# Four buffers for block 0 of the probabilities, and a narrower tile for the last two key blocks of P^T

## The chip, the cores and the metric

The kernel runs on one core of one Trainium2 chip. The metric is the device time of one execution in microseconds (us). The core has a matrix engine (PE, with the loading of its weights as a row of its own, PEld), a vector engine (DVE), a scalar engine (ACT), a general engine (POOL) and a queue that issues DMAs (SP). Each engine works through its own list of instructions in order and waits on semaphores for the others.

## The reference

Block-causal attention over 8 batches x 8 heads, 576 positions, head dimension 64, and then one feed-forward layer over the 4608 tokens whose activation is a rational function.

```python
scores = 1/sqrt(64) * q @ k.T                      # per head, 576 x 576
mask   = (i // 64) >= (j // 64)                    # blocks of 64
attn   = exp(scores - max); attn /= attn.sum + 1e-9
x      = (attn @ v) as 4608 x 512
h = x @ w_in                                       # 512 -> 2048
P = a0 + a1 h + a2 h^2 + a3 h^3
Q = 1 + |b0||h| + |b1| h^2
out = (P / (Q + 1e-6)) @ w_out                     # 2048 -> 512
```

All of it is float32. The kernel keeps that accuracy by splitting each operand into a high and a low part (names ending in h and l, of the type fp32r) and by summing three products of them, so every matrix product appears three times on PE.

## The kernel before

**Attention** goes through 32 visits, one for each pair of heads (8 batches x 4 pairs). A visit has five row blocks t = 0 to 4 with 64, 128, 128, 128, 128 queries that see 64, 192, 320, 448, 576 keys. For each t and each of the two heads, `scores` (L414 to L441) multiplies q by k on PE and takes the row maxima on DVE; where t > 0 a matmul of 64 columns (L436) adds the mask to the last 64 keys. `expo` (L443) takes the exponential on ACT (L449), and when both heads are there POOL scales the rows by 1/sum: keys 0 to 63 of both heads go to a small tile `pk` (L458, "block 0"), the other keys stay in place (L462).

`transp` (L466 to L488) transposes the probabilities on PE in groups of blocks, one PSUM bank a group (L481). From each group ACT copies the high part (L486) and DVE takes the low part (L487) into tiles that live through the whole attention: `pt0` (block 0 of t = 0, 1, 2), `pt1` (blocks 1 to 4 of t = 1, 2) and `pt2` (blocks 0 to 8 of t = 3, 4: nine key blocks by 256 queries, the first 128 of t = 3 and the second 128 of t = 4). The queries of t = 3 see 448 keys, which are blocks 0 to 6; for blocks 7 and 8 their columns are zeroed once at the start (L323) and stay zero.

`pv` (L490) multiplies V by these tiles. Its second group (g = 1) is nine key blocks by three products, 27 matmuls of 256 columns, six of them on blocks 7 and 8 (L500). ACT and DVE split the result (L503, L504), and a DMA writes it to DRAM as x.

**The feed-forward part** is cut in two passes. The first does 10 of the 16 slices of the inner dimension for 18 chunks of 256 tokens, five units a chunk: unit `c_u` is unit u of chunk c. In a unit, `first` makes 24 matmuls (L207), then ACT, POOL (L216, L217) and DVE evaluate P and Q, `recip` and `split` end in gh on ACT (L239) and gl on POOL (L240), and `second` makes 12 matmuls with these as weights (L257). The second pass does the other six slices for chunks of 512 tokens and runs after attention.

**Order.** The program emits attention item by item and feed-forward steps between them by a fixed count. What emits first has priority, but the list that each engine gets is settled by the framework's scheduler, which places an instruction when, on its own timeline, its inputs are there and its tile has a free buffer. `pk` has two buffers (L420): the pk of row block t can be written only after the transposes of the row block two before it have read theirs, and `transp` follows its row block by 9 or 10 items, about a visit.

Of the kernel before, what the change touches and what calls it, by code (L numbers as in the profile page):

```python
# [9 lines left out]
F32 = mybir.dt.float32  # L10
F32R = mybir.dt.float32r
# [50 lines left out]
def attn_ffn_kernel(  # L62
# [11 lines left out]
    nc = tc.nc  # L74
# [32 lines left out]
    b0, b1 = bab[:, 0:1], bab[:, 1:2]  # L107
# [197 lines left out]
    Q0 = [0, 64, 192, 320, 448]  # L305
# [3 lines left out]
    with ExitStack() as actx:  # L309
        ps_a = actx.enter_context(tc.tile_pool(name="ps_a", bufs=5, space=PSUM))  # L310
        att = actx.enter_context(tc.tile_pool(name="att", bufs=2))
        apers = actx.enter_context(tc.tile_pool(name="apers", bufs=1))


        pt0 = [apers.tile([128, 1, 320], F32R, name=f"pt0{x}") for x in "hl"]
        pt1 = [apers.tile([128, 4, 256], F32R, name=f"pt1{x}") for x in "hl"]
        pt2 = [apers.tile([128, 9, 256], F32R, name=f"pt2{x}") for x in "hl"]

        vpad = [apers.tile([128, 128 + 4 * 192], F32R, name=f"vp{x}") for x in "hl"]
        for x in pt1:  # L320
            nc.vector.memset(x[:, 2:4, 0:128].bitcast(F32), 0.0)
        for x in pt2:
            nc.vector.memset(x[:, 7:9, 0:128].bitcast(F32), 0.0)  # L323
        for x in vpad:
            nc.vector.memset(x.bitcast(F32), 0.0)

# [69 lines left out]
        def vblock(x, b):  # L396
            c = 0 if b == 0 else 128 + 192 * ((b - 1) // 2) + 64 * ((b - 1) % 2)
            return x[:, c:c + 128]
# [3 lines left out]
        def bank(p, name):  # L402

            if p < LEND:
                nbank[0] += 1
                pool, tag = ((ps_a, "a"), (ps_o, "o0"), (ps_o, "o1"), (ps_h, "a"))[nbank[0] % 4]
            else:
                pool, tag = ps_a, "a"
            return pool.tile([128, 512], F32, name=name, tag=tag)

        def pieces(t):
            return [(0, NK[t])] if t < 4 else [(0, 288), (288, 288)]

        def scores(p, t, j):  # L414
            s = st_[p]
            nq = NQ[t]
            if j == 0:
                pt = att.tile([128, 2, NK[t]], F32, name=f"p{p}_{t}", tag=f"p{t}", bufs=1)

                pk = att.tile([128, 2, 64], F32, name=f"pk{p}_{t}", tag="pk", bufs=2) if t > 0 else pt  # L420
                nm = att.tile([128, 2, 2], F32, name=f"nm{p}_{t}", tag="nm", bufs=4)
                sm = att.tile([128, 2, 2], F32, name=f"sm{p}_{t}", tag="sm", bufs=4)
                s[t] = (pt, pk, nm, sm)
            pt, pk, nm, sm = s[t]
            kq = s["kq", j]
            qs = slice(Q0[t], Q0[t] + 128)
            banks = []
            for i, (c0, w) in enumerate(pieces(t)):
                ww = max(w, 256)
                ps = ps_a.tile([128, 512], F32, name=f"s{p}_{t}_{j}_{i}", tag="a")  # L430
                last = t > 0 and c0 + w == NK[t]
                nc.tensor.matmul(ps[:, :ww], lhsT=kq[:, 0, qs], rhs=kq[:, 1, c0:c0 + ww], start=True, stop=False)  # L432
                nc.tensor.matmul(ps[:, :ww], lhsT=kq[:, 0, qs], rhs=kq[:, 2, c0:c0 + ww],  # L433
                                 start=False, stop=not last)
                if last:
                    nc.tensor.matmul(ps[:, w - 64:w], lhsT=mrow, rhs=mcol, start=False, stop=True)  # L436
                nc.vector.reduce_max(out=nm[:nq, j, i:i + 1], in_=ps[:nq, :w], axis=AX.X, negate=True)  # L437
                banks.append(ps)
            if t == 4:
                nc.vector.tensor_tensor(out=nm[:, j, 0:1], in0=nm[:, j, 0:1], in1=nm[:, j, 1:2], op=ALU.min)  # L440
            s[t, j] = banks  # L441
# [24 lines left out]
        def transp(p, t):  # L466
            pt, pk, _, _ = st_[p].pop(t)
            nq = NQ[t]
            nb = 1 + 2 * t
            groups = {1: [1], 3: [1, 2], 5: [1, 4], 7: [4, 3], 9: [3, 3, 3]}[nb]  # L470
            blk = 0
            for gi, gn in enumerate(groups):
                ps = bank(p, f"t{p}_{t}_{gi}").rearrange("p (c t) -> p c t", c=4)
                for i in range(gn):
                    x = blk + i
                    if x == 0:
                        src = pk[:nq].rearrange("q j k -> q (j k)")
                    else:
                        key = 64 + 128 * ((x - 1) // 2)
                        src = pt[:nq, (x - 1) % 2, key:key + 128]  # L480
                    nc.tensor.transpose(ps[:, i, :nq], src, ident[:nq, :nq])  # L481
                (hi, lo), b0, c0 = ((pt2, blk, Q0[t] - 320) if t > 2 else (pt0, 0, Q0[t]) if blk == 0 else
                                    (pt1, blk - 1, Q0[t] - 64))
                dh = hi[:, b0:b0 + gn, c0:c0 + nq]
                dl = lo[:, b0:b0 + gn, c0:c0 + nq]
                nc.scalar.copy(out=dh, in_=ps[:, :gn, :nq])  # L486
                nc.vector.tensor_tensor(out=dl, in0=ps[:, :gn, :nq], in1=dh.bitcast(F32), op=ALU.subtract)  # L487
                blk += gn  # L488

        def pv(p, g):  # L490
            b, hp = divmod(visits[p][0], NPAIR)
            vh, vl = vpad
            nb, w = ((5, 320), (9, 256))[g]
            o = ps_a.tile([128, 512], F32, name=f"o{p}_{g}", tag="a")
            for x in range(nb):
                s0 = 64 if (g == 0 and x > 0) else 0
                hi, lo = ((y[:, x] for y in pt2) if g else (y[:, 0] for y in pt0) if x == 0 else
                          (y[:, x - 1] for y in pt1))
                for i, (vv, pp) in enumerate(((vh, lo), (vh, hi), (vl, hi))):
                    nc.tensor.matmul(o[:, s0:w], lhsT=vblock(vv, x), rhs=pp,  # L500
                                     start=(x == 0 and i == 0), stop=(x == nb - 1 and i == 2))
            xs = att.tile([128, 2, 320], F32R, name=f"x{p}_{g}", tag="xs", bufs=1)
            nc.scalar.copy(out=xs[:, 0, :w], in_=o[:, :w])  # L503
            nc.vector.tensor_tensor(out=xs[:, 1, :w], in0=o[:, :w], in1=xs[:, 0, :w].bitcast(F32), op=ALU.subtract)  # L504
            nc.sync.dma_start(out=xscr[b][:, hp, :, g * 320:g * 320 + w], in_=xs[:, :, :w].bitcast(F32))
# [7 lines left out]
        def attn_steps():  # L513
# [8 lines left out]
            for k in range(len(items) + ALAG2 + ALAG3 + 8):  # L522
                for x in [x for x in todo if x[0] == k]:
                    todo.remove(x)
                    x[1](*x[2])
                if k < len(items):
                    p, t, j = items[k]
                    ts = visits[p][1]
                    if (t, j) == (ts[0], 0):
                        if p + 1 < NV:  # L530
                            o0, o1, o2 = OFFS[len(ts)]
                            at(k + o0, load, p + 1)
                            at(k + o1, prep, p + 1, 0)
                            at(k + o2, prep, p + 1, 1)
                    at(k + ALAG2, expo, p, t, j)
                    if j == 1:
                        lag = min(ALAG3, nxt[k] - 1)
                        at(k + lag, transp, p, t)
                        if t in (2, 4):
                            at(k + lag + 1, pv, p, t // 4)  # L540
                            if t == ts[-1] and p + 1 < NV:
                                at(k + lag + 1, vprep, p + 1)
                    scores(p, t, j)
                yield k
# [87 lines left out]
```

## Time and profile before

| | |
|---|---|
| median of 3 runs | 1382.86 us (1381.88 to 1384.80) |
| profiled execution, its own time | 1380.84 us |
| its span in the trace | 1379.1 us |
| instructions in it | 24416 |
| PE, weight load busy | 1278.1, 1149.6 us |
| DVE, ACT, POOL busy | 1027.2, 909.4, 958.2 us |
| granted PE clock, mean | 0.974 |
| DMA | 200.84 MB, mean 146 GB/s |

The profile is of one execution. A row of a group reads: line, engine, operation, output<-input, sizes and count, then busy us and mean ns of one, then idle time of the engine just before these instructions and what ended it. A row of the waits reads: who waited <- for whom, us in total, times, longest. A row of the chain or of the timeline begins with its start and its us. In names, the numbers of buffers are left out.

### The profile page before, as it was taken

What the parts mean: (1) busy time and instruction counts of PE and PEld (TensorE: products, weight loads), DVE (VectorE), ACT (ScalarE), POOL (GpSimd) and SP (SyncE); (2) the same over time, 40 slices, a digit from 0 to 9 for tenths busy, and PEclk for the clock granted to TensorE, in tenths of its full rate; (3) what the DMA queues carried; (4) which work ended last, traced back from release to release, by engine and by line L of the source; (5) the groups of instructions that cost most, each with busy time, mean ns of one, the idle gap of its engine ahead of it and who ended that gap; (6) DMA issues with size and microseconds to landing.
All of it is one profiled execution on the core that took longest, in us unless ns stands there. A gap on an engine that the chain in (4) does not pass through costs nothing.

```text
span 1379.1 us, 24416 instructions
## 1 busy us (share of the span) xinstructions
PE 1278.1 (93%) x8088; PEld 1149.6 (83%) x8088; DVE 1027.2 (74%) x2048; ACT 909.4 (66%) x2250; POOL 958.2 (69%) x1240
## 2 busy tenths in 40 slices
PE   4677899999899979999999999999989999999997
PEld 3667788999888879888998999998979888888885
DVE  5898877787778857887767777776676767676675
ACT  4766767777677756777767777776645655555553
POOL 4889987687678747777767676666556666666654
PEclk9788999999999999999999999999999999999999
DMA  9778556666556655665654555652632233333332
GB/s 216 198 196 238 146 150 166 168 166 181 148 145 150 164 151 132 165 166 153 157 140 123 154 134 122 160 127 65 213 141 77 77 123 123 122 123 123 122 113 86
DMA packets 216925, 200.84 MB, mean 146 GB/s; under 512 B 129504, under 2 KB 184800, under 8 KB 216800
## 3 DMA queue, kind: packets, MB, share of 16 engines
q1 hardware_dynamic: 216736, 199.28, 53.6%
q8 instruction: 65, 1.06, 0.3%
q14 instruction: 60, 0.49, 0.1%
q0 software_dynamic: 64, 0.00, 0.0%
HBM read 98.57 MB, written 44.04 MB: 103 GB/s over the span
## 4 chain that ended last, share of the span: by engine, by line
PE 69%; DVE 9%; POOL 9%; DMA 5%; ACT 3%; issue 3%; SPq 1%; POOLq 0%; DVEq 0%; ACTq 0%
PE h L207 25%; PE o L257 24%; PE o L500 8%; PE t L481 4%; PE s L432 3%; PE s L433 2%; PE tp L366 2%; POOL gl L240 1%; POOL p L462 1%; DMA x<-xscr 1%; POOL u L217 1%; DVE v L231 1%; DVE nm L437 1%; POOL v L216 1%; DMA xscr<-x 1%
## 5 line engine op out<-in xcount | busy, mean ns | idle before, releaser
L207 PE MATMUL h<-x,wih 128*128 128x256 f32 (+1 forms) x1872 | 415.7, 313 | 9.0 <-DMA x<-xscr 7.9
L207 PEld LDWEIGHTS h<-x,wih 128*128 128x128 f32 x1872 | 309.7, 191 | 29.1 <-issue 6.6
L207 PE MATMUL h<-x,wil 128*128 128x256 f32 (+1 forms) x936 | 290.7, 311 | 0.0
L240 POOL TENSOR_TENSOR gl<-s,gh 128x512 fp32r<-128x512 f32 x144 | 188.8, 1313 | 106.4 <-ACT gh L239 103.0
L257 PE MATMUL o<-woh,gl 128*128 128x512 f32 x576 | 232.2, 403 | 12.1 <-POOL gl L240 10.6
L257 PE MATMUL o<-wol,gh 128*128 128x512 f32 x576 | 227.7, 396 | 0.0
L257 PE MATMUL o<-woh,gh 128*128 128x512 f32 x576 | 227.7, 395 | 0.0
L437 DVE TENSOR_REDUCE nm<-s 128x1 f32<-128x288 f32 (+4 forms) x384 | 161.7, 427 | 78.4 <-PE s L436 45.2
L449 ACT ACTIVATE p<-s,nm 128x288 f32<-128x288 f32 (+4 forms) x384 | 184.9, 485 | 48.3 <-DVE nm L437 35.0
L217 POOL TENSOR_TENSOR u<-v,u 128x512 f32<-128x512 f32 x144 | 189.6, 1317 | 9.8
L216 POOL TENSOR_SCALAR v<-u,bab 128x512 f32<-128x512 f32 x144 | 118.9, 826 | 98.1 <-ACT u L214 94.6
L207 PEld LDWEIGHTS h<-x,wil 128*128 128x128 f32 x936 | 178.7, 191 | 8.7
L462 POOL TENSOR_SCALAR p<-p,rc 128x128 f32<-128x128 f32 (+3 forms) x256 | 164.8, 655 | 29.6 <-DVE rc L457 27.7
L218 DVE TENSOR_TENSOR s<-s,h 128x512 f32<-128x512 f32 x144 | 98.5, 684 | 100.1 <-ACT s L215 99.4
L432 PE MATMUL s<-kq 128*128 128x256 f32 (+3 forms) x384 | 137.3, 360 | 24.3 <-DMA kq<-hl 8.9
L224 ACT ACTIVATE v<-u,qcb 128x512 f32<-128x512 f32 x144 | 104.6, 726 | 69.6 <-POOL u L217 68.9
L214 ACT ACTIVATE u<-h 128x512 f32<-128x512 f32 x144 | 85.9, 596 | 94.2 <-PE h L207 90.1
L239 ACT CAST gh<-s 128x512 fp32r<-128x512 f32 x144 | 89.2, 623 | 82.1 <-DVE s L232 81.5
L257 PEld LDWEIGHTS o<-woh,gl 128*128 128x128 f32 x576 | 109.2, 190 | 35.5 <-POOL gl L240 14.3
L257 PEld LDWEIGHTS o<-wol,gh 128*128 128x128 f32 x576 | 109.1, 189 | 22.2
L257 PEld LDWEIGHTS o<-woh,gh 128*128 128x128 f32 x576 | 109.3, 190 | 18.9
L433 PE MATMUL s<-kq 128*128 128x256 f32 (+3 forms) x384 | 120.1, 315 | 0.0
(105 smaller groups left out, 3043.5 us busy)
## 6 DMA issues: line engine op xcount, KB each, us to landing
kq<-hl SPq DMA_DIRECT2D x64, 432.0 KB, 4.3
kq<-hl SPq DMA_DIRECT2D x64, 288.0 KB, 5.3
x<-xscr SPq DMA_DIRECT2D x56, 256.0 KB, 4.2
xscr<-x SPq DMA_DIRECT2D x32, 320.0 KB, 4.7
qr<-in_q_dram SPq DMA_DIRECT2D x64, 144.0 KB, 2.9
kr<-in_k_dram SPq DMA_DIRECT2D x64, 144.0 KB, 3.0
kq<-hl SPq DMA_DIRECT2D x64, 144.0 KB, 4.8
pscr<-os SPq DMA_DIRECT2D x18, 512.0 KB, 2.9
```

The lines of the kernel that those rows point to most:

```text
L207: nc.tensor.matmul(h[:, j, :], lhsT=w[:, dc, fs], rhs=xs[dc][:, hl, :], start=(dc == 0 and i == 0), stop=(dc == 3 and i == 2))
L216: nc.gpsimd.tensor_scalar(out=vt, in0=ut, scalar1=b1, scalar2=b0, op0=ALU.mult, op1=ALU.add)
L217: nc.gpsimd.tensor_tensor(out=ut, in0=vt, in1=ut, op=ALU.mult)
L224: nc.scalar.activation(out=vt, in_=ut, func=AF.Ln, bias=qcb)
L240: nc.gpsimd.tensor_tensor(out=gl.rearrange("p j t -> p (j t)"), in0=st, in1=gh.rearrange("p j t -> p (j t)").bitcast(F32), op=ALU.subtract)
L257: nc.tensor.matmul(self.o[m], lhsT=g[:, j, ms], rhs=w[:, f, :], start=(u == 0 and j == 0 and i == 0), stop=(u == nu - 1 and j == NBU[ph] - ...
L432: nc.tensor.matmul(ps[:, :ww], lhsT=kq[:, 0, qs], rhs=kq[:, 1, c0:c0 + ww], start=True, stop=False)
L433: nc.tensor.matmul(ps[:, :ww], lhsT=kq[:, 0, qs], rhs=kq[:, 2, c0:c0 + ww], start=False, stop=not last)
L437: nc.vector.reduce_max(out=nm[:nq, j, i:i + 1], in_=ps[:nq, :w], axis=AX.X, negate=True)
L449: nc.scalar.activation(out=pt[:nq, j, c0:c0 + w], in_=banks[i][:nq, :w], func=AF.Exp, bias=nm[:nq, j, 0:1], scale=1.0, accum_out=sm[:nq, j ...
L462: nc.gpsimd.tensor_scalar(out=pt[:nq, jj, 64:n], in0=pt[:nq, jj, 64:n], scalar1=rc[:nq, jj:jj + 1], scalar2=1.0, op0=ALU.mult, op1=ALU.mult)
L500: nc.tensor.matmul(o[:, s0:w], lhsT=vblock(vv, x), rhs=pp, start=(x == 0 and i == 0), stop=(x == nb - 1 and i == 2))
```

## The change

`pk` gets four buffers. `pt2` shrinks to the seven blocks that both row blocks use, and blocks 7 and 8 get a tile `pt3` of 128 columns, those of t = 4; the two memsets of zeros go. The transposes of t = 4 are grouped 4, 3, 2 so that the last group is what goes to `pt3`. `pv` takes blocks 7 and 8 from `pt3` with 128 columns that add to the second half of its result. Per partition, `pt2` and `pt3` together hold 2 KB less than `pt2` did, and `pk` 1 KB more.

```diff
-        pt2 = [apers.tile([128, 9, 256], F32R, name=f"pt2{x}") for x in "hl"]
+        pt2 = [apers.tile([128, 7, 256], F32R, name=f"pt2{x}") for x in "hl"]
+        pt3 = [apers.tile([128, 2, 128], F32R, name=f"pt3{x}") for x in "hl"]
...
-        for x in pt2:
-            nc.vector.memset(x[:, 7:9, 0:128].bitcast(F32), 0.0)
...
-                pk = att.tile([128, 2, 64], F32, name=f"pk{p}_{t}", tag="pk", bufs=2) if t > 0 else pt
+                pk = att.tile([128, 2, 64], F32, name=f"pk{p}_{t}", tag="pk", bufs=4) if t > 0 else pt
...
-            groups = {1: [1], 3: [1, 2], 5: [1, 4], 7: [4, 3], 9: [3, 3, 3]}[nb]
+            groups = {1: [1], 3: [1, 2], 5: [1, 4], 7: [4, 3], 9: [4, 3, 2]}[nb]
...
-                (hi, lo), b0, c0 = ((pt2, blk, Q0[t] - 320) if t > 2 else (pt0, 0, Q0[t]) if blk == 0 else
+                (hi, lo), b0, c0 = ((pt3, 0, 0) if blk == 7 else (pt2, blk, Q0[t] - 320) if t > 2 else (pt0, 0, Q0[t]) if blk == 0 else
...
-                s0 = 64 if (g == 0 and x > 0) else 0
-                hi, lo = ((y[:, x] for y in pt2) if g else (y[:, 0] for y in pt0) if x == 0 else
-                          (y[:, x - 1] for y in pt1))
+                pt, b0, s0 = (((pt2, x, 0) if x < 7 else (pt3, x - 7, 128)) if g else
+                              (pt0, 0, 0) if x == 0 else (pt1, x - 1, 64))
+                hi, lo = (y[:, b0] for y in pt)
```

The scheduler also settles a new order on every engine. Three places of it follow; the lines from L500 on are one higher in the changed kernel, and the last number of a name counts tiles.

The first is POOL in the second visit, one piece of the difference: `rc` is 1/sum of a row block (the number behind the name is t), `sm` the sums, `wao`, `wai`, `wil` and `wol` belong to the splitting of the weights, `vpl` is the low part of V.

```order
 L458 TENSOR_TENSOR pk_2_467<-p_2_466,rc_2_535 128x128
 L462 TENSOR_SCALAR p_2_466<-p_2_466,rc_2_535 128x256 x2
+L458 TENSOR_TENSOR pk_3_542<-p_3_541,rc_3_575 128x128
 L462 TENSOR_SCALAR p_3_541<-p_3_541,rc_3_575 128x384 x2
 L145 TENSOR_TENSOR wil_143<-wpi_2_2_1416,wai_2_2_1414 128x2x256
 L394 TENSOR_TENSOR vpl<-vr_204,vph 128x4x64 x2
+L130 TENSOR_SCALAR wao_2_1458<-wao_2_1458 128x512
 L455 TENSOR_TENSOR sm_4_584<-sm_4_584 128x2
-L458 TENSOR_TENSOR pk_3_542<-p_3_541,rc_3_575 128x128
```

The pk of t = 3 now stands right behind the row block before it, ahead of its own p rows; before, it stood behind them and behind rows of the weights and of V.

The second is PE at the last visit's transposes of t = 4 (`t_4_0`, `t_4_1`, `t_4_2` are the three groups, `h_14_1` and `h_15_1` feed-forward units). Before:

```order
L481 MATMUL t_3_1_13441<-ident,p_3_13098 128x128
L481 MATMUL t_4_0_13485<-ident,pk_4_13177 128x128
L481 MATMUL t_4_0_13485<-ident,p_4_13176 128x128 x2
L481 MATMUL t_4_1_13491<-ident,p_4_13176 128x128 x3
L481 MATMUL t_4_2_13497<-ident,p_4_13176 128x128 x3
L207 MATMUL h_15_1_13875<-x_15_0_13751,wih_142 128x256 x2
```

And in the changed kernel:

```order
L481 MATMUL t_3_1_13441<-ident,p_3_13098 128x128 x3
L481 MATMUL t_4_0_13485<-ident,pk_4_13177 128x128
L481 MATMUL t_4_0_13485<-ident,p_4_13176 128x128 x3
L481 MATMUL t_4_1_13492<-ident,p_4_13176 128x128 x3
L207 MATMUL h_14_1_13556<-x_14_1_13345,wih_142 128x256
L207 MATMUL h_14_1_13556<-x_14_1_13345,wil_143 128x256
L481 MATMUL t_4_2_13498<-ident,p_4_13176 128x128 x2
```

The groups hold 4, 3 and 2 blocks instead of 3, 3 and 3, and the feed-forward unit beside them is an earlier one.

The third is PE at the last P·V of all (`o_1`), with the second product of a feed-forward unit ahead of it (`o_14_1` is the sum of chunk 14; the numbers of gl and gh name the unit). Before:

```order
L257 MATMUL o_14_1_13738<-woh_144,gl_14_3_13817 128x512
L257 MATMUL o_14_1_13738<-woh_144,gh_14_3_13816 128x512
L257 MATMUL o_14_1_13738<-wol_145,gh_14_3_13816 128x512
L500 MATMUL o_1_13520<-pt2l,vph 128x256
L500 MATMUL o_1_13520<-pt2h,vph 128x256
L500 MATMUL o_1_13520<-pt2h,vpl 128x256
```

And in the changed kernel, where the six matmuls on blocks 7 and 8 come apart from the other 21:

```order
L257 MATMUL o_14_1_13738<-woh_144,gl_14_0_13608 128x512
L257 MATMUL o_14_1_13738<-woh_144,gh_14_0_13607 128x512
L257 MATMUL o_14_1_13738<-wol_145,gh_14_0_13607 128x512
L501 MATMUL o_1_13520<-pt3l,vph 128x128
L501 MATMUL o_1_13520<-pt3h,vph 128x128
L501 MATMUL o_1_13520<-pt3h,vpl 128x128
```

The last P·V now stands behind unit 14_0, three units earlier than before.

## The prediction

> **What bounds the kernel now.** I read three views in this order: busy time by stage, the chain that ended last, and the waits of the engine that the chain names. First the stages: up to 200 us (attention alone, with the weights being split), 200 to 1000 (attention mixed with the first pass of the feed-forward part), and the rest (feed-forward alone). Columns: stretch and its length, then busy us and instructions of each engine, granted clock, DMA share, GB/s.
>
> ```profile
> core 0: us, PE busy (x) PEld busy (x) DVE busy (x) ACT busy (x) POOL busy (x), PEclk, DMA share, GB/s
> 0.00:200.00 200.00, 145.47 (x905) 131.30 (x906) 162.92 (x373) 133.90 (x385) 163.00 (x218) 0.87 0.76 193
> 200.00:1000.00 800.00, 767.59 (x5489) 712.93 (x5487) 606.64 (x1311) 569.71 (x1534) 570.91 (x827) 1.00 0.59 150
> 1000.00:1379.00 379.00, 365.07 (x1698) 305.39 (x1698) 257.62 (x366) 205.79 (x332) 224.29 (x196) 0.98 0.33 112
> ```
>
> From 200 us on PE is busy 96% of the time at full clock; in the first stage DVE and POOL are busier (163 of 200) than PE (145). So PE work taken away counts after 200 us and hardly before, and of PE's idle time only 800 - 767.6 = 32.4 us is there to be won in the middle stage. The chain says the same:
>
> ```profile
> PE 69%; DVE 9%; POOL 9%; DMA 5%; ACT 3%; issue 3%; SPq 1%; POOLq 0%; DVEq 0%; ACTq 0%
> PE h L207 25%; PE o L257 24%; PE o L500 8%; PE t L481 4%; PE s L432 3%; PE s L433 2%; PE tp L366 2%; POOL gl L240 1%; POOL p L462 1%; DMA x<-xscr 1%; POOL u L217 1%; DVE v L231 1%; DVE nm L437 1%; POOL v L216 1%; DMA xscr<-x 1%
> ```
>
> The P·V matmuls (L500) are 8% of it, so a cheaper L500 shows in the end; POOL is 9%.
>
> **Part 1: six matmuls of each second P·V group stream 128 columns, not 256.** What a 256-column matmul costs is the step from start to start, not its recorded duration (the records overlap). PE's timeline (start, duration):
>
> ```profile
> 806.24 0.19 PE L436 MATMUL s<-mcol,mrow 128*128 128x64 f32 x1
> 806.26 0.36 PE L500 MATMUL o<-pt2l,vph 128*128 128x256 f32 x1
> 806.47 0.28 PE L500 MATMUL o<-pt2h,vph 128*128 128x256 f32 x1
> 806.58 0.29 PE L500 MATMUL o<-pt2h,vpl 128*128 128x256 f32 x1
> ...
> 808.38 0.28 PE L500 MATMUL o<-pt2h,vpl 128*128 128x256 f32 x1
> ```
>
> From 806.47 to 808.38 are 16 steps: 0.12 us each. A 128-column matmul on fp32r data is not in the trace. The nearest row is L436 with 64 columns: from its start to the second L500 is 0.23 us, and one 256-column step of that is 0.12, so 64 columns cost 0.11. A quarter of the columns saves a twelfth of the time: under 256 columns something other than streaming sets the step, in a stream of fp32r matmuls with a new weight each. So 128 columns lie between 0.11 and 0.12, and the gain between 0 and 0.01 us each; I take 0.01, the row it is nearest to in kind. How many count, from the group in the stage 200 to 1000:
>
> ```profile
> L500 PE MATMUL o<-pt2l,vph 128*128 128x256 f32 x234 | 68.1, 291 | 0.3 <-ACT p L449 0.3
> ```
>
> 234 / 9 key blocks = 26 of the 32 visits. 26 x 6 x 0.01 = **1.6 us** less. The six visits before 200 us give nothing, since PE has 54 us to spare there.
>
> The Trainium skill, "TensorE: Matmul & The Clock Gate", section "Back-to-back issue gap", gives about 81 ns for a sustained 128-column matmul with its weight load; by that (an estimate) this term would be 156 x 0.04 = 6 us. The trace has 0.11 us already at 64 columns, so it does not agree, and the measurement decides; what it would do is rival 5.
>
> Why I do not fear that a narrow fp32r matmul takes several passes (four passes over 64 columns would be as long as one over 256, and 0.11 is close to 0.12): the same L436 ahead of plain fp32 transposes is shorter.
>
> ```profile
> 801.79 0.19 PE L436 MATMUL s<-mcol,mrow 128*128 128x64 f32 x1
> 801.82 0.30 PE L481 MATMUL t<-ident,pk 128*128 128x128 f32 x1
> 801.97 1.04 PE L481 MATMUL t<-ident,p 128*128 128x128 f32 x8
> ```
>
> Eight transposes take 1.04 us from first start to last end, one lasts about 0.28, so a step is (1.04 - 0.28) / 7 = 0.11. L436 and one transpose together take 801.97 - 801.79 = 0.18, which leaves 0.07 for the 64 columns: less than four passes.
>
> **Part 2: the three transpose groups of t = 4 hold 4, 3 and 2 blocks, not 3, 3 and 3.** Nine transposes either way. The copies after them, on ACT (L486) and DVE (L487), by width (busy, mean ns of one):
>
> ```profile
> L486 ACT CAST pt2h<-t 128x384 fp32r<-128x384 f32 x128 | 60.2, 486 | 21.1 <-PE t L481 20.8
> L486 ACT CAST pt2h<-t 128x512 fp32r<-128x512 f32 x32 | 18.8, 587 | 5.3 <-PE t L481 5.1
> L486 ACT CAST pt1h<-t 128x256 fp32r<-128x256 f32 x32 | 12.0, 374 | 2.1 <-PE t L481 1.9
> L487 DVE TENSOR_TENSOR pt2l<-t,pt2h 128x384 fp32r<-128x384 f32 x128 | 68.8, 547 | 3.9 <-ACT pt2h L486 3.7
> L487 DVE TENSOR_TENSOR pt2l<-t,pt2h 128x512 fp32r<-128x512 f32 x32 | 21.8, 683 | 2.1 <-ACT pt2h L486 2.0
> L487 DVE TENSOR_TENSOR pt1l<-t,pt1h 128x256 fp32r<-128x256 f32 x32 | 13.3, 415 | 2.0 <-ACT pt1h L486 1.8
> ```
>
> ACT: 3 x 486 = 1458 before, 587 + 486 + 374 = 1447 ns after; DVE: 1641 before, 1645 after. Nothing. The first group is ready some 0.1 + 0.1 + 0.14 us later (one more transpose, copy and subtraction) and the last as much earlier; the L500 group above waits 0.3 us in all over 26 visits, so neither counts. The two removed memsets (0.27 us each, on DVE at the start) lie beside the load of k, which the chain has there (start, us):
>
> ```profile
> L323 DVE MEMSET pt2h<- 128x256 f32 x1 | 0.3, 272 | 0.0
> 2.27 4.32 DMA kr<-in_k_dram
> ```
>
> Without that cover they would cost 0.5 us; I count nothing.
>
> **Part 3: four buffers for pk.** With two, the row that writes pk (L458) stands on POOL until transposes of two row blocks back have read it. POOL's waits in 200 to 1000, then PE's and the weight load's there (total, times, longest), then the same pk wait in 0 to 200:
>
> ```profile
> POOL pk L458 <- PE t L481: 42.5, 32, 4.3
> POOL gl L240 <- ACT gh L239: 30.3, 24, 4.1
> ...
> PE o L257 <- POOL gl L240: 5.8, 7, 1.4
> ...
> PEld o L257 <- POOL gl L240: 8.3, 11, 1.6
> ...
> POOL pk L458 <- PE t L481: 0.3, 1, 0.3
> ```
>
> So 42.5 us of POOL's idle time go. But POOL sits idle for 800 - 570.9 = 229 us of that stage, and PE waits for it only at gl, for 5.8 us or, if all the loads' waits are others, 5.8 + 8.3 = 14.1. If pk's share of POOL's idle time (42.5 / 229 = 0.19) is its share in these waits, that is 1.1 to 2.6 us. The chain bears out that it is little: a pk that PE released stands in it twice, at 31 us (its wait is the 0.3 above) and here (start, us, what):
>
> ```profile
> 636.93 0.12 PE t L481
> 637.05 0.07 issue
> 637.12 0.81 POOL pk L458
> ```
>
> I take **1.8 us**; the ends are 0 and 14.1. Nothing waits anew: POOL's later rows and PE's are only let go earlier. What is late next on POOL is gl waiting for ACT (30.3 us).
>
> **Part 4: the order.** A different readiness of pk reorders all five queues. At the end of attention PE has the second product of unit 14_0 ahead of the last P·V where it had 14_3: three units move behind attention. A unit's first product is 24 matmuls and its second 12 (chain rows), and 2.88 + 2.75 = 5.6 us, so 17 us of PE work. The stretch right behind attention is a little worse than the middle stage (60.1 of 66 us busy at clock 0.95, against 0.96 at 1.00):
>
> ```profile
> 965.91 2.88 PE h L207 x24
> ...
> 981.53 2.75 PE o L257 x12
> ```
>
> ```profile
> 984.00:1050.00 66.00, 60.08 (x380) 54.34 (x379) 43.00 (x51) 34.42 (x56) 38.86 (x32) 0.95 0.49 176
> ```
>
> 17 x (1 / (0.91 x 0.95) - 1 / 0.96) = 2 us lost, if that stretch stays as it is; as likely it is a fixed passage that does not grow. I take 0, and keep -6 to +9 for the order as a whole: the gain a fifth of the 32.4 us of PE's idle time, the loss that of rival 3.
>
> **Sum.** The profiled execution took 1380.84 us (span 1379.1): 1380.84 - 1.6 - 1.8 = 1377.4. It lies 2.0 under the median of the three runs, 1382.86, in whose terms I forecast **1379.4**, with 1376 to 1381 as the forecast's own range.
>
> **Rivals.** A measurement of this kernel can tell some 0.2%, 2.8 us, from no change: faster is under 1380.1, slower over 1385.6.
>
> 1. The forecast, chance 0.40.
> 2. Nothing arrives, 0.25: the 128-column step is 0.12 like that of 256, and POOL, let go by pk, waits for ACT's gh instead. For it: those 30.3 us, and POOL's 229 idle us. Time 1382.9.
> 3. Slower, 0.22: pk no longer holds POOL back, so pk and its two p rows run ahead of a gl for which PE is waiting. Rows: pk 505 ns, p 655, gl 1313:
>
> ```profile
> L458 POOL TENSOR_TENSOR pk<-p,rc 128x128 f32<-128x128 f32 x128 | 64.5, 505 | 46.9 <-PE t L481 42.8 <-DVE rc L457 2.2
> L462 POOL TENSOR_SCALAR p<-p,rc 128x128 f32<-128x128 f32 (+3 forms) x256 | 164.8, 655 | 29.6 <-DVE rc L457 27.7
> L240 POOL TENSOR_TENSOR gl<-s,gh 128x512 fp32r<-128x512 f32 x144 | 188.8, 1313 | 106.4 <-ACT gh L239 103.0
> ```
>
> Each hit makes PE's L257 late by 0.5 + 2 x 0.65 = 1.8 us. Four hits decide ((2.8 + 3.4) / 1.8); with five the time is 1379.4 + 9 = 1388. For it: already 18 waits for gl. Against: they last 0.8 us each, so most gl have a lead.
> 4. Narrow matmuls take four passes, 0.03: 192 x (2 x 0.12 - 0.12) = 23 us, 1405. Against: the 0.07 above.
> 5. The step falls with the columns, 0.03: 156 x 0.06 = 9.4 in place of 1.6, 1371.6. Against: 0.11 at 64 columns.
> 6. The new order also fills PE's idle 54 us before 200, 0.07: the first feed-forward units stand earlier on PE; a tenth of it gives 1374. Against: POOL and DVE, at 82%, have little room.
>
> **Range and chances.** 1371 to 1390 leaves out rival 4, the worst quarter of rival 3 and the far ends of 5 and 6: about 0.12. Faster: 0.40 + 0.03 + 0.07, less 0.04 for the forecast's upper end: 0.46. Same: 0.25 + 0.04 = 0.29. Slower: 0.22 + 0.03 = 0.25.
>
> **What would show it.** On PE's timeline a 128-column L501 step of 0.11 (right), 0.06 (rival 5) or 0.24 (rival 4). The pk wait for transposes near 0, with POOL's waits for ACT grown by most of 42.5 us. PE's waits for gl fallen by 1 to 3 us (right), the same (rival 2) or grown, with pk and p rows right before a late gl (rival 3). The forecast is wrong if PE's idle time between 200 us and the end of attention moves by over 5 us either way.

## The result, and the profile after

The changed kernel takes **1400.54 us** (median, 1398.90 to 1401.62), the kernel before beside it 1383.83 (1381.88 to 1386.36): 1.0121 times as long, 95% interval 1.0105 to 1.0138. The forecast was 1379.4 with a range of 1371 to 1390. The time moved the other way and lies outside the range.

The stages of the changed kernel (profiled execution 1401.54 us, span 1399.8), in the columns of the table by stage in the prediction:

```profile
0.00:200.00 200.00, 145.21 (x871) 130.95 (x872) 153.56 (x364) 132.20 (x373) 158.31 (x213) 0.85 0.74 188
200.00:1000.00 800.00, 764.47 (x5383) 704.93 (x5383) 586.89 (x1300) 558.93 (x1523) 556.10 (x820) 0.98 0.59 151
1000.00:1400.00 400.00, 385.03 (x1836) 323.44 (x1834) 271.63 (x384) 217.86 (x354) 241.10 (x208) 0.99 0.32 107
```

In the middle stage PE made 5383 matmuls where it had made 5489, POOL worked 556 us instead of 571, and the granted clock is 0.98 instead of 1.00. The shares of the chain moved from PE to the engines around it (PE had 69%, DVE and POOL 9% each, DMA 5%):

```profile
PE 64%; DVE 11%; POOL 9%; DMA 7%; ACT 4%; issue 3%; SPq 2%; POOLq 0%; DVEq 0%; ACTq 0%
```

POOL's waits from 200 to 1000 us (total, times, longest) show what came in place of the 42.5 us for the transposes:

```profile
POOL rc L456 <- ACT p L449: 58.3, 41, 4.3
POOL gl L240 <- ACT gh L239: 52.0, 24, 5.7
POOL pk L458 <- DVE rc L457: 34.5, 53, 2.7
```

In the kernel before, rc and the first user of rc waited there:

```profile
POOL rc L456 <- ACT p L449: 28.6, 29, 2.4
POOL p L462 <- DVE rc L457: 27.7, 59, 1.7
```

The wait of pk for PE's transposes has fallen from 42.5 us to 1.8, as forecast. But rc (the sum plus 1e-9, for which the exponential must be done) now waits 58.3 us instead of 28.6, pk waits 34.5 us for DVE's reciprocal of rc, and gl 52.0 instead of 30.3. Each of them holds whatever stands behind it in POOL's list. Whether that is what the kernel pays for is tested below.

How much work was lost, and where, shows best against a kernel that differs in one number: experiment e2 below is the changed kernel with two pk buffers, span 1375.3 us. First e2's rows, then those of the changed kernel, by stretch (same columns):

```profile
0.00:200.00 200.00, 146.32 (x896) 132.65 (x897) 155.84 (x371) 131.76 (x377) 158.19 (x215) 0.84 0.76 191
200.00:960.00 760.00, 735.78 (x5239) 682.44 (x5239) 575.47 (x1279) 547.63 (x1505) 555.83 (x813) 0.99 0.59 149
```

```profile
200.00:960.00 760.00, 729.18 (x5144) 672.78 (x5143) 565.66 (x1264) 537.33 (x1481) 537.22 (x799) 0.98 0.59 148
```

By 960 us e2 has made 896 + 5239 = 6135 of its 8088 matmuls, the changed kernel 871 + 5144 = 6015. What is left takes the same pace: 1953 in 415.3 us (0.213 us each), 2073 in 439.8 (0.212). So all of the 24.5 us between the two spans are there by 960, and the 120 matmuls are worth 25 us: some 5 from before 200, 20 from the mixed stage. What is missing is feed-forward work, as the gl group from 200 to 1000 shows, e2 first:

```profile
L240 POOL TENSOR_TENSOR gl<-s,gh 128x512 fp32r<-128x512 f32 x74 | 97.0, 1310 | 14.3 <-ACT gh L239 12.4 <-PE o L501 1.4 <-DMA kq<-hl 0.2
```

```profile
L240 POOL TENSOR_TENSOR gl<-s,gh 128x512 fp32r<-128x512 f32 x70 | 90.4, 1292 | 55.1 <-ACT gh L239 52.0 <-DVE rc L457 1.5 <-PE o L501 0.7
```

74 units against 70; at the 5.6 us of PE a unit (the prediction's Part 4) that is 22 us. Attention's last P·V ends at 974.5 us in e2 and at 977.9 in the changed kernel (979.7 before). So attention is hardly later; the loss is feed-forward units that no longer fit beside it and are made up behind it.

### The profile page after: what moved, and what is told of

Read it like the earlier page. It is cut to its first block, busy times and chain, and to the rows that moved or that the text cites. A ratio compares the mean times of both kernels' runs of the same rounds, so it can differ in the third digit from the quotient of the medians.

```text
span 1399.8 us, 24489 instructions
## 1 busy us (share of the span) xinstructions
PE 1294.7 (92%) x8088; PEld 1159.3 (83%) x8088; DVE 1012.1 (72%) x2046; ACT 909.0 (65%) x2250; POOL 955.5 (68%) x1240
## 4 chain that ended last, share of the span: by engine, by line
PE 64%; DVE 11%; POOL 9%; DMA 7%; ACT 4%; issue 3%; SPq 2%; POOLq 0%; DVEq 0%; ACTq 0%
PE o L257 23%; PE h L207 23%; PE o L501 7%; PE t L481 4%; DMA kq<-hl 4%; PE s L432 3%; PE s L433 3%; POOL gl L240 2%; PE tp L366 2%; POOL u L217 1%; POOL v L216 1%; DVE nm L437 1%; DVE u L230 1%; DVE v L231 1%; DVE s L232 1%
## 5 line engine op out<-in xcount | busy, mean ns | idle before, releaser
L207 PE MATMUL h<-x,wih 128*128 128x256 f32 (+1 forms) x1872 | 415.3, 313 | 13.7 <-DVE s L219 8.2
L257 PE MATMUL o<-woh,gl 128*128 128x512 f32 x576 | 236.0, 410 | 9.7 <-POOL gl L240 9.5
L257 PE MATMUL o<-woh,gh 128*128 128x512 f32 x576 | 230.7, 400 | 0.0
L257 PE MATMUL o<-wol,gh 128*128 128x512 f32 x576 | 229.6, 399 | 0.0
L432 PE MATMUL s<-kq 128*128 128x256 f32 (+3 forms) x384 | 141.6, 371 | 31.6 <-DMA kq<-hl 21.0
L257 PEld LDWEIGHTS o<-woh,gl 128*128 128x128 f32 x576 | 111.3, 193 | 33.9 <-POOL gl L240 13.4
L257 PEld LDWEIGHTS o<-wol,gh 128*128 128x128 f32 x576 | 111.1, 193 | 23.4
L257 PEld LDWEIGHTS o<-woh,gh 128*128 128x128 f32 x576 | 111.3, 193 | 19.4
L481 PE MATMUL t<-ident,p 128*128 128x128 f32 (+1 forms) x672 | 114.8, 281 | 10.8 <-ACT p L449 3.0
```

Of the source, the lines that this page charges most:

```text
L207: nc.tensor.matmul(h[:, j, :], lhsT=w[:, dc, fs], rhs=xs[dc][:, hl, :], start=(dc == 0 and i == 0), stop=(dc == 3 and i == 2))
L257: nc.tensor.matmul(self.o[m], lhsT=g[:, j, ms], rhs=w[:, f, :], start=(u == 0 and j == 0 and i == 0), stop=(u == nu - 1 and j == NBU[ph] - ...
```

## The experiments

Eighteen kernels, each timed over three rounds against the kernel before on the same chip (its median was 1382.2 to 1384.0 beside all of them). The ratio is to that kernel, with its 95% interval.

**Which part of the change costs?** e1 is the kernel before with the groups alone; e2 is the changed kernel with two pk buffers; e3 has three.

```diff
# e1, against before
-            groups = {..., 9: [3, 3, 3]}[nb]
+            groups = {..., 9: [4, 3, 2]}[nb]
# e2, against after (e3 has bufs=3)
-                pk = att.tile(..., tag="pk", bufs=4) if t > 0 else pt
+                pk = att.tile(..., tag="pk", bufs=2) if t > 0 else pt
```

> Only the transposes of t = 4 are regrouped 4, 3, 2; pt2 keeps nine blocks of 256 columns and pk its two buffers. Theory A (the loss is made by pk's four buffers, whose rows stand on POOL where they wait for the softmax of their own row block): within 3 us of the kernel before. Theory B (the loss comes with any new order of the queues, whatever the cause of it): 5 to 20 us slower.

> The narrow tile and the groups, pk back at two buffers. Theory A: within 4 us of the kernel before (the six narrow matmuls save 1.6 us). Theory B: 5 to 20 us slower. Theory C (the narrow tile itself costs): about 17 us slower, like the whole change.

> The whole change, but pk with three buffers. Theory A: between the two-buffer kernel and the whole change, 4 to 14 us slower than before. Theory B: anything from 0 to 20 us slower, in no order with the number of buffers. Theory C: about 17 us slower.

Measured: e1 1376.10 us, 0.9958 (0.9942 to 0.9975); e2 1376.33, 0.9960 (0.9947 to 0.9974); e3 1384.55, 1.0017 (1.0001 to 1.0032). So groups and narrow tile together win 6 us, and against e2 the pk buffers lose 8 with three and 24 with four (by the ratios 8 and 22). Theory A has the order of the numbers right, but it foresaw neither the gain of e1 and e2 nor how little e3 loses against the kernel before (2 us, not 4 to 14). B and C are out with e1 and e2. e2's POOL waits from 200 to 960 us:

```profile
POOL p L462 <- DVE rc L457: 36.0, 63, 1.7
POOL pk L458 <- PE t L481: 33.1, 27, 3.4
POOL sm L455 <- ACT p L449: 31.3, 16, 4.3
POOL rc L456 <- ACT p L449: 25.3, 30, 2.0
```

With two buffers the first user of rc is mostly the p row, and pk waits for PE; with four, pk is mostly the first user and POOL waits at rc and pk.

**Is it the number of feed-forward units left over?** The program meters them by a count of steps, in which `UP` sets the pace of the first units and `HOLD` the feed-forward steps kept back for after attention. e4, e6 and e8 let the four-buffer kernel do 74 units before the last P·V, as many as the kernel before does (after has 71); e5 makes the kernel before do only 71. e7 leaves the count alone and emits the feed-forward steps one item earlier against attention (`ALAG3`; the transposes follow their row block by 9 items as it is, except in the last visit, where it was 10).

```diff
# e4, e6, e7, e8, against after
-UP = 25
+UP = 30
...
-                           (UN * UP // 100 + (U1 - UN * UP // 100) * (step - E0 - UN + 1) // (E1 + KB - E0 - UN)))
+                           (UN * UP // 100 + 6 + (U1 - UN * UP // 100) * (step - E0 - UN + 1) // (E1 + KB - E0 - UN)))
...
-ALAG3 = 10
+ALAG3 = 9
...
-HOLD = 6
+HOLD = 3
# e5, against before
-HOLD = 6
+HOLD = 12
```

> The whole change, with the feed-forward steps emitted faster in the first stretch (30 per 100 items, not 25), after which 74 units' second products stand on PE ahead of the last P.V, as before the change, and not 71. Theory A: POOL still waits where pk stands, 10 to 17 us slower than before. Theory D (what is lost is the feed-forward work that no longer fills attention): within 5 us of the kernel before.

> The kernel before (two pk buffers) with the feed-forward steps emitted six later (HOLD 12): 71 units' second products ahead of the last P.V, as few as in the changed kernel. Theory D (three units fewer inside attention are the loss, whoever takes them out): 10 to 17 us slower than before. Theory A (four pk buffers are the loss): within 4 us of before.

> The whole change with six feed-forward steps more from the end of the first stretch on: 74 units ahead of the last P.V, four pk buffers. Theory D: 1379 to 1386, back by 15 us or more. Theory A: 1390 to 1400, since POOL's pk rows stand where they did.

> The whole change with ALAG3 = 9, which only moves the feed-forward steps one item earlier against attention: another order, four pk buffers, 71 units ahead of the last P.V. Theories A and D: 1394 to 1402. Theory B (the changed kernel has an unlucky order): anywhere from 1376 to 1400.

> The whole change with HOLD 3: three feed-forward steps more by the end of attention, 74 units ahead of the last P.V, four pk buffers. Theory D: 1379 to 1388. Theory A: 1390 to 1400. Theory B: no relation to the units.

Measured: e4 1388.31 (1377.79 to 1391.90), 1.0036 (1.0015 to 1.0056); e5 1383.53, 1.0009 (0.9998 to 1.0020); e6 1403.17, 1.0158 (1.0143 to 1.0173); e7 1406.16, 1.0173 (1.0150 to 1.0197); e8 1392.34, 1.0095 (1.0059 to 1.0130). e5 leaves three units more and loses nothing: its last P·V ends at 963.6 us, 16 earlier than in the kernel before. e6 leaves none more and is as slow as the changed kernel: its last P·V ends at 997.0, 19 later than there. In e6, units put in ahead of attention's end are paid for there.

No theory gives all five. e4, which D wanted within 5 us of the kernel before and A 10 to 17 us slower, is 5 or 6 us slower, so 12 faster than the changed kernel; its executions spread over 14 us. e8, with its 74 units, lies in A's range; its median is 8 us below the changed kernel's, but the intervals overlap. e6, with as many, wins nothing; e7 is slower than every theory had it. So the number of units left behind attention does not by itself set the time, though another order with more of them can win a part of the loss back, as e4 does.

**Can the order be mended by holding POOL's rows back?** In POOL's list the pk of the changed kernel stands within two rows of its rc in 106 of 128 row blocks, in e2 in 23 of 128. Five kernels with four buffers feed a [128, 2] or [128, 1] value, 0 times a row maximum, into rc (e9) or into what pk and p read (e11), so that these rows can't be placed before the next row block's maximum; e10 is the control of e9, with the row block's own maximum. e17 delays pk alone and leaves p early; e18 is meant as its control, but differs in a second thing: e9, e10, e11 and e17 also emit the held rows two items later, and e18 does not. e16 gives the maxima (`nm`) two buffers instead of four, so that scores bunch less.

```diff
# e9 (e10 has src = nm), against after
+            ep = att.tile([128, 1], F32, name=f"ep{p}_{t}", tag="ep", bufs=4)
+            src = st_[p][t + 1][2] if t < 4 else nm
+            nc.vector.tensor_scalar(out=ep[:nq], in0=src[:nq, 1, 0:1], scalar1=0.0, scalar2=1e-9,
+                                    op0=ALU.mult, op1=ALU.add)
-            nc.gpsimd.tensor_scalar_add(rc[:nq], sm[:nq, :, 0], 1e-9)
+            nc.gpsimd.tensor_scalar(out=rc[:nq], in0=sm[:nq, :, 0], scalar1=ep[:nq, 0:1], scalar2=1.0,
+                                    op0=ALU.add, op1=ALU.mult)
# e11, ahead of pk and p; e17, ahead of pk alone (e18 has nx = nm); r0 is the rc of before
+            pt, pk, nm, r0 = st_[p][t]
+            nx = st_[p][t + 1][2] if t < 4 else nm
+            rc = att.tile([128, 2], F32, name=f"rd{p}_{t}", tag="rd", bufs=4)
+            nc.vector.scalar_tensor_tensor(out=rc[:nq], in0=nx[:nq, :, 0], scalar=0.0, in1=r0[:nq],
+                                           op0=ALU.mult, op1=ALU.add)
# where they are emitted: norm in e9, e10 and e11, late in e17; e18 has late and 0 in place of 2
+                        at(k + ALAG2 + 2, norm, p, t)
# e16, against after
-                nm = att.tile(..., tag="nm", bufs=4)
+                nm = att.tile(..., tag="nm", bufs=2)
```

> The whole change with four pk buffers, and the 1e-9 that is added to the row sums taken from a value that depends on the next row block's maxima (nm of t + 1 times 0 plus 1e-9; one small DVE row more for each row block): rc, pk and p on POOL become ready one row block later in the scheduler's timeline. Theory A1 (with four buffers POOL's rows of the softmax stand so early that POOL waits for ACT's exponential, 58 us at rc where it was 25 to 33 with two): the rc waits on ACT fall below 35 us and the time comes back to 1378 to 1390. Theory A2 (four buffers are slow for another reason): 1395 to 1408.

> The control of the run before: the same extra DVE row, but made from the row block's own maxima, so that nothing is delayed. Theories A1 and A2: 1395 to 1408, like the whole change, with rc waits on ACT of 50 us or more.

> As e9, but the dependency on the next row block lies between 1/sum and its users: rc stays where it was on POOL, and pk and p come one row block later (28 of 128 pk rows within two rows of their rc, where the whole change has 106 and the kernel before 17). Theory A1: POOL still waits at rc, 1392 to 1408. Theory A3 (what costs is pk and p right behind rc, waiting for DVE's reciprocal): back to 1376 to 1388.

> The whole change (four pk buffers) with two buffers instead of four for the row maxima nm, which holds the scores back instead of pk: on PE's list a quarter of the runs of five scores hold less than 10.3 us of PE work, as with two pk buffers, where the whole change has 9.6. Theory S (four pk buffers let the scores bunch, and PE runs dry between the bunches): 1376 to 1388. Otherwise 1390 to 1406.

> After, four pk buffers, with only the pk row of POOL held until the row maximum of the next row block (a [128, 2] operation on DVE, 0 times that maximum added to rc, feeds pk alone); the two p rows keep reading rc and stay early. In the order, pk then stands within two POOL rows of its rc in 12 of 128 row blocks and 5.2 rows behind it on average, as in the kernel before (17 of 128, 5.6), where after had 106 of 128 and 2.0. Theory P (the place of the pk rows on POOL is what costs: pk straight behind rc holds POOL for DVE's reciprocal): 1376 to 1388, and POOL's wait of pk for rc falls from 34.5 us to under 10. Rival (pk's place is not it; four buffers let the whole softmax chain bunch): 1393 to 1405 as in all orders with four buffers so far.

> Control for e17: the same added [128, 2] operation on DVE, but with the row block's own maximum, so that pk is only one DVE operation later (within two POOL rows of rc in 44 of 128, 3.2 rows on average). Theory P: between e17 and after, 1385 to 1402. Rival: as e17, 1393 to 1405. If e17 and e18 differ by less than 4 us and both lie near 1400, what in the order costs the time stays open.

Measured: e9 1399.37, 1.0126 (1.0085 to 1.0166); e10 1402.49, 1.0141 (1.0108 to 1.0174); e11 1399.77, 1.0116 (1.0087 to 1.0145); e16 1395.50, 1.0095 (1.0077 to 1.0113); e17 1396.17, 1.0084 (1.0053 to 1.0115); e18 1386.44, 1.0019 (1.0007 to 1.0032). Holding rows back does not win the time back: A1 (in e9), A3 (e11), S (e16) and P (e17) each miss the time they asked for. (e10 also missed its row: its rc waits 27.9 us for ACT, where 50 or more was expected.) e17 puts pk where the kernel before has it (within two rows of rc in 12 of 128, before 17), and its theory asked for at most 1388; its POOL waits from 200 to 1000 us say that the waits only changed place:

```profile
POOL rc L456 <- ACT p L449: 36.2, 26, 4.4
POOL p L460 <- DVE rc L457: 34.5, 47, 3.3
POOL v L216 <- ACT u L214: 26.4, 22, 4.1
POOL gl L240 <- ACT gh L239: 25.9, 19, 5.3
POOL pk L472 <- DVE rd L470: 25.9, 27, 2.4
```

e18 is 10 us faster than e17, with the largest rc wait of all kernels with pk on POOL and 0.9 us of wait for pk's new input; whether the maximum that is read or the place of emission makes the 10 us is not shown:

```profile
POOL rc L456 <- ACT p L449: 72.0, 48, 4.4
POOL p L460 <- DVE rc L457: 37.8, 58, 2.9
POOL gl L240 <- ACT gh L239: 35.1, 17, 5.0
```

e4 says the same. Its profiled execution is its fastest, 1377.79 us, as fast as e2's, and yet has these waits from 200 to 1000 us:

```profile
POOL rc L456 <- ACT p L449: 52.4, 36, 3.4
POOL pk L458 <- DVE rc L457: 41.3, 63, 2.9
```

So neither the place of pk nor the total of one wait predicts the time: both of my theories about a single row fell. e18 and e4 also show that four buffers do not force 1400.

**Is it the memory, the groups' direction, or POOL?** e13 is e2 with pk tiles twice as wide of which half is used: the memory of four buffers, with the instructions of every engine in e2's order. e12 is the kernel before with groups 2, 3, 4. e14 and e15 put the pk row on DVE, with four and with two buffers.

```diff
# e13, against e2
-                pk = att.tile([128, 2, 64], ..., bufs=2) if t > 0 else pt
+                pk = att.tile([128, 4, 64], ..., bufs=2)[:, 0:2, :] if t > 0 else pt
# e12, against before
-            groups = {..., 9: [3, 3, 3]}[nb]
+            groups = {..., 9: [2, 3, 4]}[nb]
# e14, against after; e15, against e2
-            nc.gpsimd.tensor_tensor(out=pk[:nq], in0=pt[:nq, :, 0:64],
+            nc.vector.tensor_tensor(out=pk[:nq], in0=pt[:nq, :, 0:64],
```

> The kernel before with groups of 2, 3 and 4 blocks for t = 4; two pk buffers, wide pt2. If the 6 us that the groups 4, 3, 2 won come from the place of the borders (the last copy before P.V small, borders as in t = 3): no gain here, 1381 to 1388. If any new order of this kind wins them: 1374 to 1379.

> The kernel of e2 (two pk buffers, pt3, groups 4, 3, 2) with pk tiles of twice the size of which half is used: memory and addresses as with four buffers, and the order on every engine the same as in e2. Theory L (four buffers only shift what lies behind pk in memory, and that costs): 1390 to 1400. Theory O (the order that four buffers give costs): 1374 to 1379, like e2.

> The whole change (four pk buffers) with the pk rows on DVE instead of POOL. Theory P (the place of the pk rows on POOL's list is the loss): within 6 us of e15. Theory O without P (any engine; softmax and feed-forward are dealt out otherwise on all lists): 10 to 25 us slower than e15.

> e2 (two pk buffers) with the pk rows on DVE: the pair of e14. Some 0.3 us more on DVE and 0.4 us less on POOL for each of 128 rows: 1370 to 1385.

Measured: e12 1384.10, 1.0007 (0.9990 to 1.0024); e13 1377.66, 0.9955 (0.9938 to 0.9972); e14 1395.68, 1.0096 (1.0070 to 1.0122); e15 1391.61, 1.0067 (1.0040 to 1.0094). e13 is e2 within its interval: where tiles lie in memory costs nothing here. With pk on DVE the step from two buffers to four costs 4 us, with intervals that overlap, where it costs 24 on POOL. That fits a loss that goes by POOL's list, though it is no clean proof, since e15 missed its expectation (1370 to 1385), is itself 15 us slower than e2 and may pay for the same thing in another way. e12 has no gain from the groups 2, 3, 4: not every new grouping wins.

## Why the prediction was wrong

**Part 1 (128 columns): step nearly right, gain not seen.** PE's timeline of the changed kernel (start, duration):

```profile
353.14 0.22 PE L501 MATMUL o<-pt3l,vph 128*128 128x128 f32 x1
353.20 0.28 PE L501 MATMUL o<-pt3h,vph 128*128 128x128 f32 x1
353.31 0.27 PE L501 MATMUL o<-pt3h,vpl 128*128 128x128 f32 x1
353.42 0.27 PE L501 MATMUL o<-pt3l,vph 128*128 128x128 f32 x1
353.54 0.27 PE L501 MATMUL o<-pt3h,vph 128*128 128x128 f32 x1
353.64 0.28 PE L501 MATMUL o<-pt3h,vpl 128*128 128x128 f32 x1
353.76 0.35 PE L432 MATMUL s<-kq 128*128 128x288 f32 x1
```

(353.64 - 353.31) / 3 = 0.11 us, as bounded. The first of the six is followed after 0.06 us, here and in the other visits, which the prediction did not have: the six take 353.76 - 353.14 = 0.62 us, 0.10 each, against 6 x 0.12 with 256 columns, so by this trace the term is 26 x 0.1 = 2.6 us in place of 1.6. Rivals 4 and 5 are out, and with them the 81 ns that the Trainium skill ("TensorE: Matmul & The Clock Gate", section "Back-to-back issue gap") gives for 128 columns. So small a gain could not be told apart: e2 has the narrow tile, e1 has not, and both take 1376.

**Part 2 (groups 4, 3, 2): "Nothing" was wrong by 6 us.** The rows for ACT and DVE were right; what the groups changed was the order, and behind attention. Here is the stretch from 980 to 1060 us, before and then e1:

```profile
980.00:1060.00 80.00, 74.08 (x471) 67.16 (x471) 53.56 (x65) 44.45 (x73) 46.51 (x38) 0.96 0.43 155
```

```profile
980.00:1060.00 80.00, 79.59 (x520) 72.76 (x519) 59.44 (x70) 45.27 (x75) 52.80 (x42) 1.00 0.45 162
```

PE is 5.5 us busier in e1, and the clock 0.04 higher over 80 us is worth 3 more: 8.7 us in all, against a span 4.6 us shorter and a median 6 lower. Part of it makes up for the mixed stage: by 960 us e1 has made 914 + 5168 = 6082 matmuls, the kernel before 905 + 5208 = 6113. The gap that went is one place. In PE's timeline of before (start, duration, in brackets the idle time and who ended it):

```profile
1029.84 0.80 PE L257 MATMUL o<-woh,gl 128*128 128x512 f32 x1 [3.97 <-POOL gl L240]
```

Ahead of it PE's list has 64 + 32 first-product matmuls in a row, four units, from 1014.2 us on, and then needs a gl that POOL only begins at 1028.1, when those are done:

```profile
L207 PE MATMUL h<-x,wih 128*128 128x256 f32 x64 | 11.6, 283 | 0.0
...
L207 PE MATMUL h<-x,wil 128*128 128x256 f32 x32 | 9.1, 283 | 0.0
```

e1's list alternates first and second products there, and its longest such wait in this stretch is this:

```profile
1010.05 0.50 PE L257 MATMUL o<-woh,gl 128*128 128x512 f32 x1 [0.41 <-POOL gl L240]
```

The prediction had seen this stretch and let it pass as perhaps "a fixed passage". It is not fixed. e12 keeps the gap (4.0 us) and has no gain. But e2 keeps it too (4.7 us) and is as fast as e1 all the same, since it gets on better in the mixed stage (PE busy 735.8 us from 200 to 960, e1 728.7, before 729.4; 6135 matmuls by 960, e1 6082). Two equal times with different causes: the gains of such edits can't be added.

**Part 3 (four pk buffers): the wait went, the sentence "Nothing waits anew" failed.** It holds for a fixed list: a row that is let go earlier can't make others later. The list was not fixed. Four buffers let the scheduler place pk straight behind rc (within two rows in 106 of 128 row blocks, 17 before), and in a list that is worked through in order an early place can mean waiting early, as the 34.5 us of pk for rc show. POOL's timeline in the changed kernel:

```profile
358.07 0.61 POOL L455 TENSOR_TENSOR sm<-sm 128x2 f32<-128x2 f32 x1 [1.32 <-ACT p L449]
358.77 0.22 POOL L456 TENSOR_SCALAR rc<-sm 128x2 f32<-128x2 f32 x1
359.28 0.40 POOL L458 TENSOR_TENSOR pk<-p,rc 128x128 f32<-128x128 f32 x1 [0.28 <-DVE rc L457]
359.65 1.36 POOL L462 TENSOR_SCALAR p<-p,rc 128x512 f32<-128x512 f32 x2
361.00 0.77 POOL L216 TENSOR_SCALAR v<-u,bab 128x512 f32<-128x512 f32 x1
361.73 1.30 POOL L240 TENSOR_TENSOR gl<-s,gh 128x512 fp32r<-128x512 f32 x1
```

The feed-forward rows v and gl stand behind five softmax rows (sm, rc, pk and two p), two of which wait. Part 3's check "POOL's waits for ACT grown by most of 42.5 us" came true (rc + 29.7, gl + 21.7) and was no sign of harmlessness, as I had meant it. That these waits hold the units is how I read it, not shown: e4 and e18 wait 52.4 and 72.0 us at rc, where the changed kernel waits 58.3, and lose less.

**Part 4 (order): this is the step that failed by size.** The prediction took 0 and kept -6 to +9. The order that came with four buffers measures +24 against the same kernel with two. I had counted three units pushed behind attention as 2 us, since their work is only moved; but they were pushed out because PE's time beside attention was lost, and three units are 17 us.

My own test, "PE's idle time between 200 us and the end of attention moves by over 5 us", would not have shown it. It goes from 779.7 - 749.1 = 30.6 us before to 777.9 - 746.5 = 31.4. The test counts busy time, and a matmul at half clock is busy for longer (the same L257 row lasts 0.39 us at 1013.1 us of the kernel before, at full clock, and 0.63 at 1032.1, at half). The row of the kernel before, to be read beside the changed kernel's 729.18 us, 5144 matmuls and clock of 0.98 above:

```profile
200.00:960.00 760.00, 729.41 (x5208) 677.00 (x5206) 579.72 (x1269) 544.65 (x1485) 545.58 (x801) 1.00 0.59 148
```

PE is busy for the same time and makes 64 matmuls fewer, worth 14 us at 0.212 each; 34 more are missing from before 200 us (905 against 871), worth 7: the 21 us between the two spans. In the clock records of 200 to 960 us, half clock takes 6.8 us in the kernel before and 27.3 in the changed one, which is 10 us of work; the other 4 of the 14 are in no row that I found. The prediction had priced the order by idle time and by waits for gl; the clock it priced for the stretch behind attention alone, and the mixed stage it left at 1.00.

Against e2, PE's idle time moves too: by 735.8 - 729.2 = 6.6 us from 200 to 960. The half clock takes about as much again: 13.7 us of it in e2's records of that stretch against 27.3, which is 6.8 us of work. The other 7 of the 20 us are in no row that I found. All this is of one execution of each kernel, and other executions of the kernel before took 1380.78 us at a mean clock of 0.966 and 1382.76 at 0.975; so how much of the loss the clock makes, and how much it only accompanies, stays open.

**Rival 3 had the sign, not the place.** PE's waits for gl should have grown by 9 us. They are these, PE and weight load, 200 to 1000:

```profile
PE o L257 <- POOL gl L240: 6.9, 11, 1.6
...
PEld o L257 <- POOL gl L240: 9.8, 14, 1.8
```

Before they were 5.8 and 8.3: 1 or 2 us more. As I read it, the list of PE was ordered for late units as well, so PE meets them in other places and in smaller pieces.

**What stays open.** Shown is that the loss belongs to the buffer count (e2, e3, after), that it isn't memory (e13), the narrow tile or the groups (e1, e2), or the number of units left alone (e5, e6), and that it isn't the place of pk alone (e17). In twelve kernels with four buffers the times are 1386 to 1406; in seven with two, 1376 to 1392, and 1376 to 1384 without the one that has pk on DVE. That it is the order on the engines is argued: besides it, only the earlier release of pk itself is left of a third and fourth buffer, and that would have to be tried with e2's lists and four buffers, which was not done, since the scheduler makes its own. Which feature of the order costs the time is not settled.

The best version run is e1 or e2, at 0.996 of the kernel before.

## What to carry to other kernels

A buffer more is not only a wait less: where a scheduler places instructions by readiness, it is a new list on every engine, and on an engine that works in order the row that became ready early can now wait early, in front of others. Here that is the reading that fits best, not a proof. Size such an edit by the spread of times that other orders of the same kernel give (here 8 us among orders with two buffers and 20 among those with four, found by small edits), not by the wait that it takes away, and test the edits of a change one at a time. Look also for places where PE's list has several units' first products in a row and then needs a value derived from them: that cost 4 us of idle time and 3 of clock, and one regrouping (4, 3, 2, with wide tiles) moved it away, another (2, 3, 4) did not.

## What the runs showed of the hardware

The granted clock fell here after much less than an idle stretch. Four stretches of 3.4 us in a row from the changed kernel (the columns of the table by stage):

```profile
293.20:296.60 3.40, 1.84 (x13) 1.36 (x11) 2.77 (x7) 3.03 (x11) 3.25 (x6) 1.00 0.88 205
296.60:300.00 3.40, 2.51 (x7) 1.85 (x8) 2.31 (x7) 2.32 (x9) 3.31 (x6) 0.50 0.23 80
300.00:303.40 3.40, 3.40 (x10) 2.63 (x10) 0.86 (x4) 0.87 (x2) 3.16 (x7) 0.50 0.36 82
303.40:306.80 3.40, 3.40 (x31) 3.31 (x30) 1.87 (x5) 1.79 (x6) 0.84 (x1) 1.00 0.28 64
```

A window in which PE was busy for 1.84 of 3.40 us (54%) was followed by two at half clock. Between 200 and 975 us of this kernel, every window at full clock that was followed by half clock was 30 to 68% busy; of the windows that were not, the least busy had 57%, and in the kernel before two with 49% were not. So the busy share alone gives no threshold. The Trainium skill ("TensorE: Matmul & The Clock Gate", section "What's actually happening") puts the fall behind an idle window of about 3.4 us; the length agrees, but here half a window of gaps was enough. So gaps on PE of 1.6 us in all, as in the first window, look cheap in the table of waits and can be paid for a second time.
